# Tile transposes as pairs of 64-row halves, with a new order of the five engine queues

## The chip, the cores and the metric

The kernel runs on one core of one Trainium2 chip. A core has five engines with a queue of instructions each: TensorE (PE: matmuls, with weight loads listed apart as PEld), VectorE (DVE), ScalarE (ACT), GpSimd (POOL) and SyncE (SP, which here issues the DMAs). The metric is the device time of one execution in microseconds. Before the change the median of 3 runs was 202.53 us (202.29 to 202.89).

## What is computed

A transformer layer on x of 2048 rows (tokens) by 448 columns, in bf16. First linear attention with 16 heads of 28 columns, then a gated MLP of width 1792. Cut to what matters:

```python
h  = x + attention(layernorm(x))
h2 = h + mlp(layernorm(h))

# attention
q, k, v = split(x @ wqkv)                       # 16 heads of 28
pq, pk  = q @ w_phi, k @ w_phi                  # per head
phi_q   = concat(softmax(pq), softmax(-pq))     # 56 features; phi_k likewise
kv, z   = phi_k^T @ v, sum over rows of phi_k   # over all 2048 rows
o       = (phi_q @ kv) / (phi_q @ z + 1e-6)
return o @ wo

# mlp
return (sigmoid(x @ w_gate) * (x @ w_up)) @ w_down
```

## The kernel before

**Tiles.** The rows are 16 tiles of 128 (t = 0 to 15), in four chunks of 512 (c = 0 to 3). The 448 columns are the contraction of most products. They are laid out in four blocks of 128 partitions, some of which hold 64 rows that another block repeats, and nearly all products are made as two matmuls of 64 rows that run beside each other in the upper and lower half of TensorE's array (functions `both` and `pair`, lines 304 to 323). A product of two outputs comes as an op "a" (output 1 from the lower 64 rows, output 2 from the upper) and an op "b" (the halves exchanged). The code lets b start only when a's matmuls have ended, since the two write each other's bank from the other half (`crosses`, line 74, and `needs_wait`, line 86); what stands between a and b in the queue fills that time.

**The first half.** For each tile: the layernorm's statistics (`bst`, `agg` on DVE), the reciprocal root (`pow1` on POOL), the normalized tile (`xn`, on DVE or POOL, lines 564 to 584), its transpose (`xT`), the products with the folded k weight and v weight (`ppa/ppb`, `vva/vvb` for tiles 0 to 3, `pva/pvb` from tile 4), two exponentials on ACT (`ek`, lines 669 to 673), the softmax's sum, reciprocal and product (`ss`, `rs` on DVE, `phi` on DVE or POOL, lines 674 to 689), the copy of v out of PSUM (`v1`), and the sum over tiles of phi^T v (`kva`, `kvb`, lines 691 to 703), which stays in PSUM banks 6 and 7 until tile 15 is in. The folded weights of q are made by `w2m1_0` to `w2m1_3` with 128 rows and copied by `w2e1`. The q products of a chunk are `pqa/pqb`, with exponentials `eq` on ACT (lines 711 to 723).

**The second half.** `kvz` copies the finished kv out of PSUM. For each tile `num` (line 774) makes the numerators and denominators, DVE makes from them `rsm`, `qq`, `b`, `c` and `rden` (lines 798 to 806), `o` is the quotient (DVE or POOL, lines 808 to 813), `oT` its transpose. `woa/wob` multiply by wo; for tiles 0 and 1 the residual x is added on TensorE. Then the second layernorm (`h`, `bs2`, `sq`, `ve`, `pow2`, `nm`, `hn`), its transpose `hT`, the gate and up products (`ga`, `gb`), the sigmoid as a tanh on ACT (`sig`), the product on DVE (`hh`), the down products (`dn`, `dp`, `dm`, `dl`) and the last sum (`fin`, `out`).

**Transposes.** Tiles from 4 on (xT) and from 2 on (oT, hT) are transposed by DMA, issued from SP's queue. The first ones are transposed on TensorE by `pe_transpose` (lines 533 to 541): four transposes of 128 by 128 into one PSUM bank, and one copy from there into SBUF by ACT or DVE. These are xT0 to xT3, oT0, oT1, hT0 and hT1, each an op of its own with its copy `xT0e` and so on.

**What sets the order.** The program is a graph of named ops (class `Graph`, line 19). Each op names what it reads and writes, and from that come the semaphores between engines. The order of each engine's queue is written out by hand in `ORDER` (lines 223 to 288), a list of names for each engine; some ops can stand on either of two engines, and the list that names them decides. An engine never passes an op that waits. Two ops, `wwo` and `wgu` (line 896), emit no instruction and only hold the waits for the wo and for the gate and up weights. `PACE` (line 289) adds one more wait: the load `ld_wg1` on SP waits for `kva14`, and as SP's queue is in order, so do the loads behind it.

Of the kernel before, what the change touches and what calls it, by code (L numbers as in the profile page):

```python
# [18 lines left out]
class Graph:  # L19
# [90 lines left out]
    def emit(self, nc):  # L110
# [85 lines left out]
P = 128  # L196
# [83 lines left out]
    ),  # L280
    "pool": (
# [753 lines left out]
```

## Time and profile before

| | |
|---|---|
| runs before | 202.29, 202.53, 202.89 us |
| the profiled execution | 202.7 us, of which 200.8 us from its first to its last instruction (the span) |
| granted TensorE clock | 1.000 over the span |
| instructions | 5854 |
| DMA | 16.26 MB in 32490 packets |
| DMA transposes, issue to landing (median) | xnT<-xn_pad 2.6 us, oT<-o_pad 2.5 us, xnT<-hn_pad 2.5 us |

The times in the profile count from the first instruction. A row of a timeline gives the start, the duration, the engine, the line of the code, the operation, and output<-inputs by the program's names with their shapes; rows of the same kind that follow each other are merged with their count. In square brackets stands how long the engine had been idle and what ended it. A row of the chain gives start, length and what ran: the chain is followed back from the last instruction to whatever released each step. Matmuls are pipelined: one of 512 columns lasts some 0.35 us from its start to its end, but the next starts much sooner, so that the distance from start to start tells what a group costs. The line of nearly all matmuls is 309, that of the helper `both`, so the names of the tiles tell them apart; line 538 is `pe_transpose`, line 531 the copy out of PSUM.

### The profile page before, as it was taken

What the parts mean: (1) busy time and instruction counts of PE and PEld (TensorE: products, weight loads), DVE (VectorE), ACT (ScalarE), POOL (GpSimd) and SP (SyncE); (2) the same over time, 40 slices, a digit from 0 to 9 for tenths busy, and PEclk for the clock granted to TensorE, in tenths of its full rate; (3) what the DMA queues carried; (4) which work ended last, traced back from release to release, by engine and by line L of the source; (5) the groups of instructions that cost most, each with busy time, mean ns of one, the idle gap of its engine ahead of it and who ended that gap; (6) DMA issues with size and microseconds to landing.
All of it is one profiled execution on the core that took longest, in us unless ns stands there. A gap on an engine that the chain in (4) does not pass through costs nothing.

```text
span 200.8 us, 5854 instructions
## 1 busy us (share of the span) xinstructions
PE 195.5 (97%) x2516; PEld 114.4 (57%) x2516; DVE 132.0 (66%) x308; ACT 89.4 (45%) x174; POOL 56.2 (28%) x95
## 2 busy tenths in 40 slices
PE   7999999999999999999999999999999999999995
PEld 4835556565568778787444444555555555554443
DVE  5999999978888986576569877346332422272224
ACT  2668988898883451434232432324323212222220
POOL 5779948633343207510170110001400000000000
PEclk9999999999999999999999999999999999999999
DMA  6965346749984230360015220020312000004002
GB/s 157 316 140 129 54 83 76 221 144 302 309 206 66 52 57 15 66 82 3 0 29 124 56 42 10 20 58 26 65 38 52 0 3 2 0 3 137 0 3 91
DMA packets 32490, 16.26 MB, mean 81 GB/s; under 512 B 24720, under 2 KB 31568, under 8 KB 32464
## 3 DMA queue, kind: packets, MB, share of 16 engines
q1 hardware_dynamic: 32336, 15.86, 33.7%
q8 instruction: 20, 0.33, 0.7%
q14 instruction: 6, 0.05, 0.1%
q10 hardware_dynamic: 128, 0.03, 0.1%
HBM read 8.34 MB, written 1.84 MB: 51 GB/s over the span
## 4 chain that ended last, share of the span: by engine, by line
PE 92%; ACT 3%; DMA 2%; issue 1%; SPq 1%; DVE 0%
PE psum L309 84%; PE psum L954 5%; DMA wk_sb<-in_A_wqkv_dram 2%; ACT hhT L671 1%; ACT eq L721 1%; ACT hhT L672 1%; PE psum L524 1%; PE psum L538 1%; PE psum L612 1%; SPq L413 1%; PE psum L599 0%; ACT xnT L531 0%; ACT v L531 0%; DVE x_sb L961 0%
## 5 line engine op out<-in xcount | busy, mean ns | idle before, releaser
L309 PE MATMUL psum<-xnT,wu_sb 64*128 64x512 bf16 (+1 forms) x490 | 93.6, 333 | 0.0
L309 PE MATMUL psum<-xnT,wg_sb 64*128 64x512 bf16 (+1 forms) x490 | 93.5, 333 | 0.1
L925 ACT ACTIVATE sg_sb<-psum 128x512 bf16<-128x512 f32 x56 | 33.2, 596 | 90.1 <-PE psum L309 89.5
L926 DVE SCALAR_TENSOR_TENSOR hhT<-sg_sb,psum 128x512 bf16<-128x512 bf16 x56 | 37.7, 684 | 52.1 <-ACT sg_sb L925 51.7
L309 PEld LDWEIGHTS psum<-xnT,wg_sb 64*128 64x128 bf16 x490 | 44.6, 94 | 20.9 <-DVE hhT L926 2.5
L309 PEld LDWEIGHTS psum<-xnT,wu_sb 64*128 64x128 bf16 x490 | 44.7, 94 | 13.9
L309 PE MATMUL psum<-wd_sb,hhT 64*128 64x448 bf16 x336 | 37.3, 349 | 0.0
L309 PEld LDWEIGHTS psum<-wd_sb,hhT 64*128 64x128 bf16 x336 | 17.8, 94 | 14.2 <-DVE x_sb L836 0.5
L309 PE MATMUL psum<-Wk,xnT 64*128 64x448 bf16 x112 | 22.2, 350 | 0.5 <-ACT hhT L672 0.2
L309 PE MATMUL psum<-wv_sb,xnT 64*128 64x448 bf16 x112 | 22.3, 351 | 0.1
L810 POOL TENSOR_TENSOR o_pad<-c_sb,rden 128x448 bf16<-128x448 bf16 x11 | 10.2, 935 | 28.5 <-DVE rden L806 28.4
L675 DVE TENSOR_REDUCE ss<-hhT 128x32 f32<-128x896 bf16 x16 | 16.8, 1060 | 0.2 <-ACT hhT L672 0.2
L721 ACT ACTIVATE eq<-psum 120x1024 bf16<-120x1024 f32 x16 | 15.6, 1030 | 0.6 <-PE psum L309 0.4
L685 POOL TENSOR_TENSOR phi<-hhT,rs 128x896 bf16<-128x896 bf16 x8 | 13.6, 1710 | 5.6 <-DVE rs L681 3.4
L309 PE MATMUL psum<-xnT,Wq 64*120 64x512 bf16 x112 | 14.8, 383 | 0.3 <-ACT eq L721 0.2
L845 POOL TENSOR_SCALAR ve<-ssq 128x1 f32<-128x1 f32 x11 | 2.2, 201 | 41.8 <-ACT junk L842 41.5
L309 PE MATMUL psum<-wo_o,oT 64*128 64x448 bf16 x56 | 13.2, 350 | 0.0
L309 PE MATMUL psum<-wo_e,oT 64*128 64x448 bf16 x56 | 13.2, 349 | 0.0
L961 DVE SCALAR_TENSOR_TENSOR x_sb<-psum,x_sb 128x448 bf16<-128x448 f32 (+2 forms) x17 | 9.4, 592 | 2.9 <-PE psum L954 1.6
L954 PE MATMUL psum<-wd_sb,hhT 128*128 128x448 bf16 (+2 forms) x70 | 11.2, 316 | 0.0
L309 PEld LDWEIGHTS psum<-Wk,xnT 64*128 64x128 bf16 x112 | 7.8, 94 | 5.8 <-PE psum L309 1.0
L671 ACT ACTIVATE hhT<-psum 128x448 bf16<-128x448 f32 x16 | 8.8, 553 | 4.4 <-PE psum L309 4.2
(105 smaller groups left out, 234.4 us busy)
## 6 DMA issues: line engine op xcount, KB each, us to landing
out_dram<-x_sb SPq DMA_DIRECT2D x15, 112.0 KB, 1.8
x_sb<-in_A_x_dram SPq DMA_DIRECT2D x7, 224.0 KB, 4.2
wd_sb<-in_B_w_down_dram SPq DMA_DIRECT2D x7, 224.0 KB, 5.1
wg_sb<-in_B_w_gate_dram SPq DMA_DIRECT2D x3, 448.0 KB, 5.8
wu_sb<-in_B_w_up_dram SPq DMA_DIRECT2D x3, 448.0 KB, 5.7
wv_sb<-in_A_wqkv_dram SPq DMA_DIRECT2D x2, 224.0 KB, 4.7
wk_sb<-in_A_wqkv_dram SPq DMA_DIRECT2D x2, 196.0 KB, 4.1
wo_e<-in_A_wo_dram SPq DMA_DIRECT2D x1, 336.0 KB, 3.3
```

Source lines behind the costliest of these rows:

```text
L309: p = e.matmul(o, lhsT=w, rhs=r, start=st, stop=sp, tile_position=(row, 0))
L413: return op(eng, name, lambda e: e.dma_start(dst, src), r=r, w=w, dma="in" if eng == "sp" else "ain", nring=48 if eng == "sp" else 8, kb=kb)
L671: e.activation(ek[:, s, :, 0, :], src, ACT.Exp)
L675: op("dve", "ss%d" % t, lambda e: e.tensor_reduce(ss[:, s, :].rearrange("p (b h) -> p b h", h=2), eks.rearrange("p b (d h) -> p b h d", h= ...
L685: return e.tensor_tensor(phi[:, sp, :, :, :].rearrange("p b a n -> p (b a) n")[:, :, 0:56].rearrange("p b (d h) -> p b d h", h=2), eks.rea ...
L721: op("act", "eq%d_%d%s" % (c, i, "pm"[sg]), lambda e, sg=sg: e.activation(eq[c][:, sg, 2 * i:2 * i + 2, :].rearrange("p g n -> p (g n)"), ...
L810: return e.tensor_tensor(o_pad[:, t % NO, off:off + D].rearrange("p (h d) -> p h d", h=H), c_sb[:, t % NS, :, 0:DH], rden[:, t % NS, :][:, ...
L845: op(("pool", "dve"), "ve%d" % t, lambda e: e.tensor_scalar(ve2[:, t:t + 1], ssq2[:, t:t + 1], 1.0 / D ** 3, EPS, op0=ALU.mult, op1=ALU.ad ...
L925: op("act", "sig" + nm, lambda e: e.activation(sg_sb[:, k, 0:W], bk(bg)[:, 0:W], ACT.Tanh, scale=0.5), r=[B(bg)], w=[("sg", k)])
L926: op("dve", "hh" + nm, lambda e: e.scalar_tensor_tensor(out=dst, in0=sg_sb[:, k, 0:W].rearrange("p (f n) -> p f n", n=N), scalar=1.0, in1= ...
L954: p = e.matmul(bk(b)[:, lo:hi], lhsT=hb[:, ff, TS(t)], rhs=wd_sb[:, ff, lo:hi], start=ff == 0, stop=ff == FT - 1)
L961: op("dve", "fin%d%s" % (t, nm), lambda e: e.scalar_tensor_tensor(out=h_sb[:, t, lo:hi], in0=bk(b)[:, lo:hi], scalar=0.5, in1=h_sb[:, t, l ...
```

## The change

Four things are changed.

1. The transposes of tiles 2 and 3 (xT2, xT3), of o tiles 0 and 1, and of hn tiles 0 and 1 are made by a new function `pair_transpose`. One op for both tiles makes 16 transposes of 64 rows by 128 columns instead of 8 of 128 by 128: the 64 lower rows of every block go to one bank, the 64 upper rows to the next, in two halves of the array. Two copies follow, one for the lower rows of both tiles, one for the upper rows. Whoever reads one of these tiles now waits for both copies. xT0 and xT1 stay as they were.
2. `ld_wg1` waits for `kva12` instead of `kva14`.
3. In SP's queue `ld_wd2` moves behind the DMA transposes oT2 and oT3, so that five down loads stand behind those and not four.
4. The queues of ACT, PE, DVE and POOL are put in another order up to about the products of tiles 4 to 7; the rest is as before. Some ops change their engine.

The functions (the keys of a tile's transposes become two, `XT(t)` and `OT(t)`, at every reader; these lines are left out):

```diff
+        def pair_transpose(names, srcs, banks, dst, rkeys, wkeys):
+            ps = [bk16(b)[:, 0:512] for b in banks]
+
+            def f(e):
+                for i, tile in enumerate(srcs):
+                    for kt, src in enumerate(tile):
+                        o = slice((i * KT + kt) * 64, (i * KT + kt + 1) * 64)
+                        for h, rows in enumerate((LO, HI)):
+                            p = e.transpose(ps[h][:, o], src[rows], ident[rows, rows], tile_position=(64 * h, 0))
+                return p
+            op("pe", names[0], f, r=["ident"] + rkeys, w=[B(b) for b in banks], rows=64, half={b: h for h, b in enumerate(banks)})
+            for h in range(2):
+                evac(names[h] + "e", dst[h], ps[h].rearrange("p (t k s) -> p t k s", t=2, k=KT), B(banks[h]), [k[h] for k in wkeys])
...
-            if t < 4:
+            if t in (2, 3):
+                if t == 3:
+                    v = xnT[0][:, :, 2 * P:4 * P].rearrange("p k (t h s) -> p h t k s", t=2, h=2)
+                    pair_transpose(("xT2", "xT3"), [[xn_pad[:, u % NX, kt * P:(kt + 1) * P] for kt in range(KT)] for u in (2, 3)], (6, 7),
+                                   [v[:, 0], v[:, 1]], [("xn", 2 % NX), ("xn", 3 % NX)], [XT(2), XT(3)])
+            elif t < 2:
...
+                if t == 1:
+                    v = oT[:, 0:2, :, :].rearrange("p t k (h s) -> p h t k s", h=2)
+                    pair_transpose(("oT0", "oT1"), [[o_pad[:, u, kt * P:(kt + 1) * P] for kt in range(KT)] for u in (0, 1)], (2, 3),
+                                   [v[:, 0], v[:, 1]], [("opad", 0), ("opad", 1)], [OT(0), OT(1)])
...
+            if t == 1:
+                v = hnT[0][:, :, 0:2 * P].rearrange("p k (t h s) -> p h t k s", t=2, h=2)
+                pair_transpose(("hT0", "hT1"), [[hn_pad[:, u, kt * P:(kt + 1) * P] for kt in range(KT)] for u in (0, 1)], (0, 1),
+                               [v[:, 0], v[:, 1]], [("hn", 0), ("hn", 1)], [XT(0), XT(1)])
...
-PACE = {"ld_wg1": "kva14"}
+PACE = {"ld_wg1": "kva12"}
```

The queues, cut to the stretches that the prediction speaks of (SP; ACT up to the exponentials of chunk 3; PE up to tile 0's gate products; the parts of DVE and POOL):

```diff
 sp:
-ld_wu3 ld_wd0 ld_wd1 ld_wd2 oT2 oT3 ld_wd3 ld_wd4 ld_wd5 ld_wd6 oT4
+ld_wu3 ld_wd0 ld_wd1 oT2 oT3 ld_wd2 ld_wd3 ld_wd4 ld_wd5 ld_wd6 oT4
 act:
-ek0 xT3e ek1 v1_0 v1_1 nm1_6 ek2 ek3 v1_2 w2e1_1 v1_3 nm1_8 w2e1_0 v1_4 ek4 w2e1_2 ek5 v1_5 w2e1_3 v1_6 ek6
+ek0 ek1 v1_1 v1_0 ek2 w2e1_1 v1_2 ek3 v1_3 w2e1_0 v1_4 ek4 ek5 v1_5 w2e1_2 w2e1_3 v1_6 ek6
...
-ek14 ek15 v1_14 v1_15 eq0_1m eq0_1p eq1_0p kvzA kvzB eq1_0m eq1_1p eq1_1m eq2_0m oT0e eq2_0p eq2_1m eq2_1p h1 h0
+ek14 ek15 v1_14 v1_15 eq0_1p eq0_1m eq1_0m kvzB kvzA eq1_0p eq1_1m eq1_1p eq2_0p oT0e oT1e eq2_0m eq2_1m eq2_1p h1 h0
 pe:
-ppa0 ppb0 warm9 xT2 xT3 vva0 vvb0 ppa2 ppb2 vva2 seed vvb2 w2m1_0 w2m1_1 kva0 pva4 kvb0 pvb4 pva5 w2m1_2 w2m1_3 pvb5
+ppa0 ppb0 warm9 xT2 vva0 vvb0 ppa2 w2m1_1 ppb2 vva2 vvb2 seed w2m1_0 w2m1_3 pva4 kva0 pvb4 pva5 kvb0 kva1 pvb5 w2m1_2
...
-pva15 kvb9 kva10 pvb15 pqa0_1 kvb10 kva11 pqb0_1 kvb11 kva12 pqa1_0 kvb12 kva13 pqb1_0 kvb13 kva14 wwo kvb14 kva15 kvb15
-qs pqa1_1 num0 num1 pqb1_1 pqa2_0 num2 pqb2_0 pqa2_1 oT0 oT1 num3 pqb2_1 woa0 wob0
-pqa3_0 num4 pqb3_0 pqa3_1 pqb3_1 num5 hT1 hT0 woa2 ga0_2 ga0_0 ga0_1 num6
+pva15 kvb9 kva10 pvb15 kvb10 kva11 pqa0_1 kvb11 kva12 pqb0_1 pqa1_0 kvb12 kva13 pqb1_0 kvb13 kva14 kvb14 kva15 kvb15
+qs pqa1_1 num0 pqb1_1 num1 pqa2_0 num2 pqb2_0 pqa2_1 oT0 pqb2_1 num3 woa0 wob0
+pqa3_0 num4 pqb3_0 pqa3_1 pqb3_1 num5 hT0 woa2 ga0_2 ga0_0 ga0_1 num6
 dve:
-bst4 xn2 agg5 agg4 agg7 bst6 xT2e agg6 ss0 bst8 rs0
+bst4 xn2 agg4 agg5 bst6 bst11 xT3e xT2e agg6 agg7 ss0 bst10 rs0
...
-rs5 xn11 ss6 xn12 rs6 ss7 phi5 phi6 xn14 rs7 ss8 ss9 rs8 ss10 rs9 ss11 rs10 ss12 v1_13 rs11 ss13 rs12 phi11 rs13 phi12
+xn11 agg15 phi3 rs5 ss7 ss6 xn12 ss8 rs6 xn14 rs7 phi6 ss9 ss10 rs8 rs9 phi8 rs10 ss11 rs11 ss12 ss13 phi11 rs12 rs13 phi12
...
-qq2 b2 c2 oT1e rsm3 rden2
+qq2 o1 b2 c2 rsm3 rden2
...
-b4 hn1 c4 hn0 rden4 rsm5 hT1e qq5 hT0e b5 c5 rsm6 rden5 qq6 b6 c6 hh0_0
+b4 c4 hn1 hn0 rsm5 qq5 hT0e hT1e rden4 b5 c5 rsm6 qq6 b6 rden5 c6 hh0_0
 pool:
-pow1_6 xn5 xn6 phi0 xn7 pow1_8 xn8 phi2 xn10 xn9 phi4 pow1_12 xn13 phi7 xn15 phi8 phi9 phi10 phi13 o0 o1 o2 o3
+pow1_6 nm1_6 xn6 xn5 phi0 xn7 nm1_8 pow1_8 phi2 xn8 xn9 xn10 phi4 pow1_12 phi5 xn13 phi7 xn15 phi9 phi10 phi13 o0 o2 o3
...
-pow2_6 pow2_5 nm5 hn5 o9 hn6 ve7 pow2_4 hn4 pow2_7 hn7
+ve6 pow2_5 pow2_4 nm5 hn4 hn5 pow2_6 o8 o9 hn6 pow2_7 hn7
```

More of the change, by code (lines that the diff above doesn't have):

```diff
@@ L531, in evac, with XT, OT @@
             op(("act", "dve"), name, (lambda e: e.copy(dst, src), lambda e: e.tensor_copy(dst, src)), r=[rkey], w=[wkey])
+        def XT(t):
+            return [("xnT", t, 0), ("xnT", t, 1)]
+        def OT(t):
+            return [("oT", t, 0), ("oT", t, 1)]
+        def pair_transpose(names, srcs, banks, dst, rkeys, wkeys):
[10 more added lines that the diff above has]
+                evac(names[h] + "e", dst[h], ps[h].rearrange("p (t k s) -> p t k s", t=2, k=KT), B(banks[h]), [k[h] for k in wkeys])
         def pe_transpose(name, srcs, bank, dst, rkey, wkey):
@@ L578, in xnorm @@
             op(("act", "dve", "pool"), "xn%d" % t, (fa, fd, fp), r=[("x", t), ("rst1", a), need], w=[("xn", s)])
-            if t < 4:
+            if t in (2, 3):
[4 more added lines that the diff above has]
+            elif t < 2:
                 pe_transpose("xT%d" % t, [xn_pad[:, s, kt * P:(kt + 1) * P] for kt in range(KT)], 6 + t % 2,
-                             xnT[0][:, :, TS(t)], ("xn", s), ("xnT", t))
+                             xnT[0][:, :, TS(t)], ("xn", s), XT(t))
             else:
                 op("sp", "xT%d" % t, lambda e: e.dma_start_transpose(out=xnT[t // 4][:, :, TS(t)], in_=xn_pad[:, s, :]),
-                   r=[("xn", s)], w=[("xnT", t)], dma="tr", nring=64)
+                   r=[("xn", s)], w=[XT(t)], dma="tr", nring=64)
         for ts in ([0], [1], [2], [3], [4, 5], [6, 7], [8, 9, 10, 11], [12, 13, 14, 15]):
@@ L654, in proj @@
             pairop("pva%d" % t, "pvb%d" % t, pair(bk(bp)[:, 0:D], bk(bv)[:, 0:D], x(t), x(t), wk2, wv),
-                   [("xnT", t)] + W2k + wv_keys, bp, bv)
+                   [XT(t)] + W2k + wv_keys, bp, bv)
         def proj2(nm, t, b, w, r):
             pairop("%sa%d" % (nm, t), "%sb%d" % (nm, t), pair(bk(b)[:, 0:D], bk(b + 1)[:, 0:D], x(t), x(t + 1), w, w),
-                   [("xnT", t), ("xnT", t + 1)] + r, b, b + 1)
+                   [XT(t), XT(t + 1)] + r, b, b + 1)
         def vcopy(t):
@@ L714, in pq @@
                           lambda h, k: xnT[c][h, k, :], lambda h, k: xnT[c][h, k, :])
-            r = W2q + [("xnT", 4 * c + j) for j in range(4)]
+            r = W2q + [XT(4 * c + j) for j in range(4)]
             op("pe", "pqa%d_%d" % (c, i), f1, r=r, w=[B(b), B(b + 1)], rows=64, half={b: 0, b + 1: 1})
@@ L819, in otrans @@
             if t < 2:
-                pe_transpose("oT%d" % t, [o_pad[:, so, kt * P:(kt + 1) * P] for kt in range(KT)], 2 + t % 2, oT[:, so, :, :],
-                             ("opad", so), ("oT", so))
+                if t == 1:
+                    v = oT[:, 0:2, :, :].rearrange("p t k (h s) -> p h t k s", h=2)
+                    pair_transpose(("oT0", "oT1"), [[o_pad[:, u, kt * P:(kt + 1) * P] for kt in range(KT)] for u in (0, 1)], (2, 3),
+                                   [v[:, 0], v[:, 1]], [("opad", 0), ("opad", 1)], [OT(0), OT(1)])
             else:
                 op("sp", "oT%d" % t, lambda e: e.dma_start_transpose(out=oT[:, so, :, :], in_=o_pad[:, so, :]),
-                   r=[("opad", so)], w=[("oT", so)], dma="tr", nring=64)
+                   r=[("opad", so)], w=[OT(so)], dma="tr", nring=64)
         def resid(t, b, ha=False):
@@ L856, in resid @@
                 op("sp", "hT%d" % t, lambda e: e.dma_start_transpose(out=hnT[c][:, :, TS(t)], in_=hn_pad[:, s, :]),
-                   r=[("hn", s)], w=[("xnT", t)], dma="tr", nring=64)
+                   r=[("hn", s)], w=[XT(t)], dma="tr", nring=64)
         def htrans(t):
-            s = t % NH
-            pe_transpose("hT%d" % t, [hn_pad[:, s, kt * P:(kt + 1) * P] for kt in range(KT)], t, hnT[0][:, :, TS(t)], ("hn", s), ("xnT", t))
+            if t == 1:
+                v = hnT[0][:, :, 0:2 * P].rearrange("p k (t h s) -> p h t k s", t=2, h=2)
+                pair_transpose(("hT0", "hT1"), [[hn_pad[:, u, kt * P:(kt + 1) * P] for kt in range(KT)] for u in (0, 1)], (0, 1),
+                               [v[:, 0], v[:, 1]], [("hn", 0), ("hn", 1)], [XT(0), XT(1)])
         def wout(t):
@@ L877, in fb @@
                             xp(t, 2, HI, False) + [(bk(2)[:, 0:D], ot(t)(HI, k), wo_e[HI, k, :], False, k == 2) for k in (0, 1, 2)])
-            r = [("oT", t % NO), ("oT", (t + 1) % NO)] + wo_keys + ([("x", t), ("x", t + 1), "ident"] if ha else [])
+            r = [OT(t % NO), OT((t + 1) % NO)] + wo_keys + ([("x", t), ("x", t + 1), "ident"] if ha else [])
             op("pe", "woa%d" % t, fa, r=r, w=[B(2), B(3)], rows=64, half={2: 0, 3: 1})
@@ L889, in part @@
                 return [(bk(b)[:, 0:D], oT[h, so, k, :], w[h, k, :], first and k == ks[0], not first and k == ks[-1]) for k in ks]
-            r = [("oT", so)] + wo_keys
+            r = [OT(so)] + wo_keys
             op("pe", "woa%d" % t, lambda e: both(e, part(LO, lo, True), []), r=r, w=[B(b)], rows=64, half={b: 0})
@@ L904, in gate_up @@
             ns = slice((t0 % 4) * P, (t0 % 4) * P + N)
-            hk = [("xnT", t) for t in range(t0, t0 + n)]
+            hk = [XT(t) for t in range(t0, t0 + n)]
             two = n == 2
```

94 rows, old and new, of the table ORDER are left out of this document.

## The prediction

> **What bounds the kernel now.** I read the page's engine rows and its chain first, then the busy time by stretch, the chain in order of time, and the timelines of TensorE, VectorE and GpSimd wherever the diff moves something. All durations are of the one profiled execution.
>
> ```profile
> PE 195.5 (97%) x2516; PEld 114.4 (57%) x2516; DVE 132.0 (66%) x308; ACT 89.4 (45%) x174; POOL 56.2 (28%) x95
> ```
> ```profile
> PE 92%; ACT 3%; DMA 2%; issue 1%; SPq 1%; DVE 0%
> ```
>
> TensorE is full and ends last, so at first sight only fewer TensorE cycles count. The stretches correct that:
>
> ```profile
> 9.00:43.40 34.40, 33.84 (x537) 19.29 (x534) 33.94 (x72) 28.82 (x66) 25.41 (x25) 1.00 0.59 131
> 43.40:58.20 14.80, 14.08 (x268) 8.49 (x262) 11.85 (x34) 13.07 (x18) 5.53 (x7) 1.00 0.93 245
> ```
>
> The columns are length, then busy time of PE, PEld, DVE, ACT and POOL. Up to 43.4 us DVE is as full as PE (33.94 of 34.40 us, 0.46 us idle). In the second stretch it is ACT (13.07 of 14.80). Two engines are close behind PE there.
>
> ```profile
> 12.32 0.48 ACT xnT L531
> ```
> ```profile
> 16.58 0.44 ACT hhT L671
> 17.02 0.44 ACT hhT L672
> 17.45 0.43 ACT v L531
> ```
> ```profile
> 47.20 1.95 ACT eq L721 x2
> ```
> ```profile
> 58.21 65.46 PE psum L309 x960
> ```
>
> The chain leaves PE for the copy of xT3, for ek3 and the copy v1_2 behind it, and for the two exponentials of pq1_1; from 58.21 us it is matmuls for 65 us without a break. What is gained before 58 us reaches the end one to one, and so does any new wait after it.
>
> **The transposes, on PE.**
>
> ```profile
> 50.20 0.62 PE L538 MATMUL psum<-ident,o_pad 128*128 128x128 bf16 x8
> 50.75 0.40 PE L309 MATMUL psum<-kvz,eq 56*128 56x60 bf16 x16
> 50.99 0.84 PE L309 MATMUL psum<-xnT,Wq 64*120 64x512 bf16 x6
> ```
> ```profile
> 57.18 0.39 PE L309 MATMUL psum<-kvz,eq 56*128 56x60 bf16 x16
> 57.59 0.62 PE L538 MATMUL psum<-ident,hn_pad 128*128 128x128 bf16 x8
> ```
>
> Starts tell PE's cost better than durations, since matmuls overlap. Eight full transposes take 50.75 - 50.20 = 0.55 us. The new pair is 16 matmuls of 64 rows and 64 columns, two row halves side by side. The trace has none of these; the nearest row is the quotient's product, 16 of 56 rows and 60 columns, 50.99 - 50.75 = 0.24 us. Before the transposes the same 16 take 57.59 - 57.18 = 0.41 us: 0.17 us is PE running empty before it goes from 64 rows to 128. So a pair saves 0.31 us, and 0.17 more where both neighbours have 64 rows: 0.48 for oT and hT, and 0.31 for xT, which still follows a 128-row warm-up. That is 1.3 us of PE; bounds are zero gain (halves one after the other) and this. How much of it ends last is settled by stage.
>
> [...]
>
> **Stage A, to the last kv product (44.4 us).**
>
> ```profile
> 17.72 0.66 ACT L629 CAST Wq<-psum 128x224 bf16<-128x224 f32 x2
> ```
>
> ACT loses the 0.48 us copy of xT3 above, and pva4 waits for v1_2 behind such a weight copy (w2e1_1, 0.66 us) where ek3 was (0.88 in the chain): 0.7 us earlier in all. PE also puts a second filler between the a and b halves of several pairs, where it waited some 0.1 us, and loses the empty wait op wwo: 0.3. PE alone could come about 1.0 us earlier. DVE can't:
>
> ```profile
> 10.63 0.40 DVE L573 TENSOR_SCALAR xn_pad<-x_sb,mv,rst 128x512 bf16<-128x512 bf16 x1
> ```
> ```profile
> 11.78 0.42 DVE L531 COPY xnT<-psum 128x512 bf16<-128x512 bf16 x1
> ```
> ```profile
> 36.53 0.62 DVE L531 CAST v<-psum 128x448 bf16<-128x448 f32 x1
> ```
> ```profile
> 42.22 1.14 DVE L685 TENSOR_TENSOR phi<-hhT,rs 128x896 bf16<-128x896 bf16 x2
> ```
> ```profile
> 43.69 0.76 PE L309 MATMUL psum<-v,phi 64*128 64x58 bf16 x24 [0.15 <-PE psum L309]
> ```
>
> DVE gains the second xT copy (0.42), gives v1_13 to ACT (0.62), and swaps phi5 for phi8 (nothing): 0.2 us less. phi15 ended at 42.22 + 1.14 = 43.36. It ends at 43.16 with the old idle time, at 42.70 with none; I take the middle, 42.95. kvb14, kva15 and kvb15 (the 24 matmuls, to 44.45) need phi14 and phi15. After phi15 at 42.95, kva15 comes at 43.2 and kvb15 ends about 43.85. **Stage A: -0.6 us**, bounds -0.1 (DVE idles 0.3 more than before) and -1.0 (PE's own).
>
> **Stage B, to the output projection woa0.**
>
> ```profile
> 49.19 1.07 PE L309 MATMUL psum<-xnT,Wq 64*120 64x512 bf16 x8 [0.25 <-ACT eq L721]
> ```
> ```profile
> 51.66 0.35 PE L309 MATMUL psum<-x_sb,ident 64*128 64x448 bf16 x2
> ```
>
> num1 moves behind pqb1_1, so the exponentials that pqa2_1 waits for start 0.24 us earlier, and the pair takes 0.48 less of PE. Against that, o1 now stands on DVE ahead of b2 and c2, whose end num3 awaits, and both oT copies stand on ACT one behind the other, 0.48 us apart as in the chain above. I work out woa0 at 51.52 where it was 51.66: **-0.14 us**, bounds 0 (ACT later by one copy) and -0.7 (all of PE's).
>
> **Stage C, to num6.**
>
> ```profile
> 57.61 0.26 DVE L798 RECIPROCAL rsm<-psum 128x16 f32<-128x16 f32 x1 [0.21 <-PE psum L309]
> 58.03 0.43 DVE L531 COPY xnT<-psum 128x512 bf16<-128x512 bf16 x1 [0.15 <-PE psum L538]
> 58.37 0.16 DVE L799 TENSOR_TENSOR qq<-rsm,psum 128x16 f32<-128x16 f32 x1
> 58.44 0.42 DVE L531 COPY xnT<-psum 128x512 bf16<-128x512 bf16 x1
> 58.78 0.63 DVE L801 TENSOR_TENSOR b_sb<-psum,qq 128x464 bf16<-128x464 f32 x1
> 59.44 0.64 DVE L804 TENSOR_TENSOR c_sb<-b_sb,psum 128x464 bf16<-128x464 bf16 x1
> ```
> ```profile
> 60.31 0.41 PE L309 MATMUL psum<-kvz,eq 56*128 56x60 bf16 x16
> ```
>
> PE would be 0.48 us early, but the copies aren't: DVE does rsm5 and qq5 (behind num5), then hT0e, hT1e, rden4, b5, c5. From num5's start, the copies end after 1.56 us (before 58.86 - 57.18 = 1.68), c5 after 2.95 (before 2.90), and num6, which needs c5's banks, comes after 3.01 instead of 60.31 - 57.18 = 3.13. **-0.12 us**, bounds +0.1 and -0.48. From num6 to the first h product DVE's row of work is the same length, since the moved rden5 fits where c6 waits for b6.
>
> **Costed at nothing.** The weight loads:
>
> ```profile
> 43.57 0.47 SPq L413 DMA_DIRECT2D wg_sb<-in_B_w_gate_dram  x1
> ```
> ```profile
> DMA to landing us min/median/max: 2.9/5.8/8.3
> ```
>
> With kva12 moved forward too, ld_wg1 and all that SP holds behind it start some 3 us earlier. The six gate and up loads of that row are issued by 46.8 and land at most 8.3 us later, 55.1; the first gate product runs at 59.01 (the row below), so nothing on PE waits for them before or after.
>
> ```profile
> 59.01 0.27 PE L309 MATMUL psum<-xnT,wg_sb 64*128 64x256 bf16 x1
> ```
>
> oT2 and oT3 go ahead of wd2 and land earlier; wd2 isn't needed before the first down products. If that cover went, woa2 would wait for oT3, and it has 0.5 us to spare, as ga0_2 behind it waits for the copies. The wgu marker moves behind products that wait for the same loads. After 58 us only order changes; PE's sum there is the same.
>
> The sum is -0.6 - 0.14 - 0.12 = -0.86 us. The profiled execution took 202.7 us (span 200.8), so 201.84 for one like it; the median of the runs, 202.53, is 0.17 lower: **201.7 us**.
>
> **Rivals.**
>
> *DVE holds stage A.* Its idle time doesn't shrink, as ss7, ss12 and ss13 now stand before older work and wait for ACT's exponentials. Then stage A gives 0.1 and the whole 0.36: 202.2. For it: DVE's fill above. Against: before, only 0.46 us of waits arose in 34.
>
> *Late transposes, slower than before.* GpSimd takes over o8 and hn4 comes ahead of o9:
>
> ```profile
> 78.05 1.21 POOL L851 TENSOR_SCALAR hn_pad<-x_sb,nm,rst 128x512 bf16<-128x512 bf16 x1 [0.18 <-POOL nm L840]
> 79.23 0.93 POOL L810 TENSOR_TENSOR o_pad<-c_sb,rden 128x448 bf16<-128x448 bf16 x1
> ```
> ```profile
> DMA to landing us min/median/max: 2.4/2.5/4.4
> ```
> ```profile
> 84.70 0.35 PE L309 MATMUL psum<-wo_e,oT 64*128 64x448 bf16 x1
> ```
>
> o9 (0.93) ends about 1.1 us later, near 81.2; its transpose is issued behind that of o8, near 81.6, and lands at 84.1 with the median of 2.5 us and at 86.0 with the longest. woa8, at 84.70, needs it: up to 1.3 us of wait, straight to the end. That is -0.86 + 1.3 = +0.44: **203.0**. It decides from a landing of 3.1 us; below that it costs nothing. For it: the longest landing and GpSimd's row of work. Against: half land within 2.5 us. The same can happen once more:
>
> ```profile
> 19.23 0.77 POOL L576 TENSOR_SCALAR xn_pad<-x_sb,nm,rst 128x512 bf16<-128x512 bf16 x1 [0.17 <-POOL rst L554]
> 20.08 1.69 POOL L685 TENSOR_TENSOR phi<-hhT,rs 128x896 bf16<-128x896 bf16 x1
> ```
>
> xn8 now stands behind phi2 and ends near 22.0 instead of 20.0; pva8, near 24.9, would wait for xT8 if that took over 2.9 us. With both the time goes past 203.1.
>
> *The halves don't run side by side.* Then 16 matmuls cost up to twice 0.24, about the old 0.55 less a little; the copies hide part: 201.9 to 202.3. Against: two row halves run together all over this trace.
>
> [...]
>
> *PE alone sets stages A to C*: the bounds -1.0 - 0.7 - 0.48 sum to -2.2; taken three quarters, since ACT's exponentials stay in B, -1.6: 200.9. For it: PE is at 97%. Against: DVE's rows.
>
> **Chances.** Forecast (201.1 to 202.2) 0.54; DVE holds A 0.15; late transposes 0.18; no side by side 0.05; PE alone 0.08. A measurement of this kernel can tell about 0.3%, 0.6 us, from no change, so faster means below 201.92: 0.45 of the forecast's 0.54, all of PE alone, a fifth of the halves rival, 0.54. Slower means above 203.14: 0.10, the half of late transposes in which both places wait. The rest is 0.36. Leaving out 0.05 below and these 0.10 above, the range is 200.9 to 203.1.
>
> **What would show it.** The pair's 16 matmuls start to next start in 0.25 us; no empty wait of 0.17 before oT and hT; DVE's last phi ends near 42.95 and num6 starts near 59.45. A DVE phi end above 43.3 refutes stage A; copies that take over 0.5 us on DVE refute stage C; a wait at woa8 for oT shows the slower rival.

## The result, and the profile after

The changed kernel takes **204.02 us** (median of 6 runs, 203.67 to 204.55), the kernel before beside it 202.50 (6 runs, 202.29 to 202.89): a ratio of 1.0074, with a 95% interval of 1.0057 to 1.0090. The change costs 1.5 us; the forecast was a gain of 0.86, and the time lies above the range. The profiled execution took 204.1 us, with a span of 202.1, at full clock. Two executions of the experiments below were in a slower state (208.17 us of a_merge19, 205.89 of a_single) and are left out of the medians and ranges.

The page of after, in the rows that answer to those of before: the engines' busy time, and the chain that ended last by engine.

```profile
PE 195.5 (97%) x2540; PEld 112.2 (56%) x2540; DVE 131.6 (65%) x305; ACT 90.1 (45%) x173; POOL 57.8 (29%) x99
PE 74%; DVE 16%; DMA 4%; ACT 2%; issue 1%; SPq 1%; DVEq 0%
```

PE is busy for the same 195.5 us, so the lost time isn't work of PE. The chain has more of DVE (16% for 0%) and of DMA (4% for 2%). The first three lines of PE's waits, longest first, name it (engine and line, what was waited for, us in total, times, longest):

```profile
PE psum L524 <- DVE zero L417: 1.2, 1, 1.2
PE psum L309 <- DMA xnT<-xn_pad: 0.9, 2, 0.5
PE psum L309 <- issue: 0.7, 1, 0.7
```

The first stands at the start of both kernels. The other two are new: PE waits twice for a DMA transpose of xn, and once for something that the view can't name. PE's timeline at these three places shows which operations they are (start, duration, and in brackets the idle time and its releaser):

```profile
22.93 0.36 PE L309 MATMUL psum<-Wk,xnT 64*128 64x448 bf16 x1 [0.42 <-DMA xnT<-xn_pad]
```
```profile
38.31 0.36 PE L309 MATMUL psum<-Wk,xnT 64*128 64x448 bf16 x1 [0.49 <-DMA xnT<-xn_pad]
```
```profile
72.05 0.35 PE L309 MATMUL psum<-wo_e,oT 64*128 64x448 bf16 x1 [0.67 <-issue]
```

They are pva7, which needs xT7, pva15, which needs xT15, and woa6, which needs oT7. Start to start, beyond the usual step (0.19 us behind such products, 0.11 behind a gate product), PE loses 0.58, 0.65 and 0.83 us there. The third releaser is a DMA too, as the landing of oT7 shows. For each kernel, the DMA view of oT7's flight (queues with packets and MB; then the issues in that stretch with their time from issue to landing), first before, 67.30 to 69.85 us:

```profile
q1 hardware_dynamic: 544, 0.13, 26.0%
issues: line engine op xcount, KB each, median us to landing
oT<-o_pad SPq DMA_TRANSPOSE x1, 2.4
```

and after, 67.8 to 72.0 us:

```profile
q1 hardware_dynamic: 1397, 0.34, 42.7%
q8 instruction: 1, 0.02, 1.4%
issues: line engine op xcount, KB each, median us to landing
oT<-o_pad SPq DMA_TRANSPOSE x1, 4.1
xnT<-hn_pad SPq DMA_TRANSPOSE x1, 2.9
```

(The last line is another transpose, hT2, which was issued behind it.) The same transpose, oT7, lands after 4.1 us where it took 2.4, and one packet of a second queue is in its flight: q8, kind "instruction". After's xT7 and xT15 show the same, 4.6 and 4.3 us for 2.5 before, each with such a packet; here the view of xT7's flight in after:

```profile
q1 hardware_dynamic: 1059, 0.26, 74.5%
q8 instruction: 1, 0.02, 2.8%
q14 instruction: 1, 0.01, 0.7%
issues: line engine op xcount, KB each, median us to landing
xnT<-xn_pad SPq DMA_TRANSPOSE x1, 4.6
```

**Where the time went, by stage.** The table gives the start of an operation's first matmul, in us of the span.

| | ppa0 | pva4 | pva8 | pva15 | kvb15 | woa0 | num6 | woa4 | woa6 | woa8 | dl15_0 |
|---|---|---|---|---|---|---|---|---|---|---|---|
| before | 9.56 | 18.02 | 25.50 | 37.76 | 44.17 | 51.66 | 60.31 | 66.44 | 69.98 | 84.70 | 197.47 |
| after | 9.16 | 17.24 | 25.13 | 38.31 | 44.64 | 52.22 | 60.87 | 66.84 | 72.05 | 86.02 | 198.78 |
| difference | -0.40 | -0.78 | -0.37 | +0.55 | +0.47 | +0.56 | +0.56 | +0.40 | +2.07 | +1.32 | +1.31 |

At ppa0 nothing of the change has run; the 0.40 us is where the second load of Wk happened to land sooner (at 5.57 us for 6.34), so the loss behind it is larger than the last column says. The other profiles below stand 0.1 to 0.5 us ahead of before at ppa0 too, all but a_pace14. (woa6 stands two gate products later in the new order, which is why a part of +2.07 is given back by woa8.) Behind woa8 the two run alike.

### The profile page after: what moved, and what is told of

The parts are those of the page before. It is cut to its first block, busy times and chain, and to the rows that moved or that the text cites. A ratio compares the mean times of both kernels' runs of the same rounds, so it can differ in the third digit from the quotient of the medians.

```text
span 202.1 us, 5905 instructions
## 1 busy us (share of the span) xinstructions
PE 195.5 (97%) x2540; PEld 112.2 (56%) x2540; DVE 131.6 (65%) x305; ACT 90.1 (45%) x173; POOL 57.8 (29%) x99
## 3 DMA queue, kind: packets, MB, share of 16 engines
q1 hardware_dynamic: 32336, 15.86, 33.7%
## 4 chain that ended last, share of the span: by engine, by line
PE 74%; DVE 16%; DMA 4%; ACT 2%; issue 1%; SPq 1%; DVEq 0%
PE psum L309 69%; PE psum L983 5%; DVE ss L700 5%; DVE st L565 4%; DMA x_sb<-in_A_x_dram 2%; DMA xnT<-xn_pad 2%; ACT eq L746 1%; DVE rs L706 1%; DVE phi L710 1%; DVE c_sb L829 1%; DVE b_sb L826 1%; DVE xnT L531 1%; SPq L413 1%; DVE xn_pad L593 1%; ACT kvz L779 1%
## 5 line engine op out<-in xcount | busy, mean ns | idle before, releaser
L309 PE MATMUL psum<-Wk,xnT 64*128 64x448 bf16 x112 | 22.7, 350 | 1.1 <-DMA xnT<-xn_pad 0.9
L309 PE MATMUL psum<-wv_sb,xnT 64*128 64x448 bf16 x112 | 22.8, 351 | 0.1
L835 POOL TENSOR_TENSOR o_pad<-c_sb,rden 128x448 bf16<-128x448 bf16 x10 | 9.6, 960 | 30.5 <-DVE rden L831 30.5
```

Source lines behind the costliest of these rows:

```text
L309: p = e.matmul(o, lhsT=w, rhs=r, start=st, stop=sp, tile_position=(row, 0))
L835: return e.tensor_tensor(o_pad[:, t % NO, off:off + D].rearrange("p (h d) -> p h d", h=H), c_sb[:, t % NS, :, 0:DH], rden[:, t % NS, :][:, ...
```

## What the instruction packets are: two theories

Queue q8 is the same on the pages of before and after:

```profile
q8 instruction: 20, 0.33, 0.7%
```

Twenty packets of 16,384 bytes are 0.33 MB. TensorE runs 2540 matmuls and as many weight loads, 5080 instructions, or 254 for each packet; the next engine, DVE, runs 305. In the same way b_merge19 below, which runs 38 instructions fewer than before (4994 for 5032), has one packet fewer:

```profile
q8 instruction: 19, 0.31, 0.6%
```

So I take q8 to be TensorE's program being fetched, a packet about every 127 matmuls (2540 / 20). The page gives q8 (0.7%) and q1, the queue of the transposes (33.7%), as shares of the same 16 DMA engines. A packet lasts about 1 us (0.93 to 1.75 in after).

**Theory F:** a fetch that falls into the flight of a DMA transpose delays its landing by up to 2 us (xT7 has 4.6 for 2.5); how it would do so no run here shows. Where the fetches fall would be set by TensorE's position in its program. Three pairs add 24 matmuls, and the order moves the transposes: so the change would have moved fetches onto transposes that PE needs at once.

**Rival O:** the new order issues these transposes later relative to their need and loads SP's queue more; long landings are chance, as before had them too (oT4 4.4, oT5 4.2, xT13 3.9 us, none of which cost PE more than 0.15). **Rival P:** the pairs themselves cost time. **Rival L:** the earlier weight loads lengthen the landings.

## The experiments

Each kernel was run beside the kernel before. The ratio is to that, with its 95% interval.

| kernel | median us | runs | ratio |
|---|---|---|---|
| b_split29 | 204.74 | 204.48 to 205.69 | 1.0110 (1.0073 to 1.0148) |
| b_pair | 204.73 | 204.52 to 207.27 | 1.0130 (1.0064 to 1.0195) |
| b_pair_merge19 | 202.40 | 202.08 to 203.34 | 0.9998 (0.9978 to 1.0019) |
| a_merge19 | 204.88 | 203.85 to 205.59 | 1.0103 (1.0052 to 1.0154) |
| a_merge19_pace14 | 202.59 | 201.74 to 203.96 | 1.0017 (0.9994 to 1.0039) |
| a_pace14 | 203.80 | 203.68 to 203.93 | 1.0070 (1.0050 to 1.0090) |
| b_merge19 | 202.73 | 202.31 to 203.56 | 1.0018 (1.0003 to 1.0033) |
| a_fill | 203.95 | 203.35 to 205.11 | 1.0080 (1.0053 to 1.0106) |
| b_split12 | 203.64 | 202.82 to 205.46 | 1.0064 (1.0037 to 1.0092) |
| a_merge14_pace14 | 202.79 | 202.40 to 204.49 | 1.0021 (1.0003 to 1.0040) |
| a_single | 202.84 | 202.46 to 203.73 | 1.0025 (1.0008 to 1.0041) |
| a_later_fold | 202.40 | 202.18 to 202.81 | 0.9990 (0.9979 to 1.0002) |

### b_split29: the kernel before, its stream 29 matmuls longer

```diff
-for i, (n, size) in enumerate(((4, 512), (1, 512), (1, 128), (2, 128), (1, 128), (6, 128), (4, 128), (6, 128), (8, 128), (2, 128))):
+for i, (n, size) in enumerate(((16, 128), (4, 128), (1, 128), (2, 128), (1, 128), (6, 128), (4, 128), (12, 64), (16, 64), (2, 128))):
```

> The kernel before, with its warm-up matmuls cut into more and smaller ones: 29 more matmuls with the same columns in all, so that everything TensorE runs behind them stands 58 instructions later in its stream. Theory F (TensorE's instruction fetches of 16 KB, one for every 256 instructions or so, delay a DMA transpose that is under way by about 1.7 us): the fetches come some 1.5 to 2 us earlier relative to the work, the one that came at 70.9 us now falls into the landing of oT7, and woa6 waits for it: 203.5 to 204.3 us, all of the loss at woa6. Rival O (the new order is what makes the waits: transposes are issued later relative to their need): nothing here changes the order, 202.3 to 202.8 us.

Measured: 204.74 us, 2.2 slower than before, though nothing but idle warm-ups was cut smaller. The chain of b_split29 in order of time, around woa6, and the DMA view of oT7's flight (67.7 to 72.0 us):

```profile
58.62 11.92 PE psum L309 x224
70.53 1.50 issue
72.03 7.97 PE psum L309 x128
```
```profile
q1 hardware_dynamic: 657, 0.16, 18.7%
q8 instruction: 1, 0.02, 1.4%
issues: line engine op xcount, KB each, median us to landing
xnT<-hn_pad SPq DMA_TRANSPOSE x2, 2.5
oT<-o_pad SPq DMA_TRANSPOSE x1, 4.2
```

woa6 waits 1.5 us for oT7, with the fetch in its flight, as F said: before's order, and after's wait. Up to pva12 (32.38 us) b_split29 stands a constant 0.37 us ahead of the profiled before, so the cut warm-ups cost nothing by themselves. Rival O had given 202.3 to 202.8. The time is above F's 203.5 to 204.3, as a second part of the loss was not expected: PE stops for half a microsecond within num0's sixteen matmuls, where no semaphore is waited for.

```profile
45.59 0.38 PE L309 MATMUL psum<-kvz,eq 56*128 56x60 bf16 x14
46.46 0.43 PE L309 MATMUL psum<-kvz,eq 56*128 56x60 bf16 x18 [0.49 <-issue]
```

### b_pair and b_pair_merge19: the pairs alone, in before's order

In b_pair the transposes are as in after, all orders as before:

```diff
-warm9 xT2 xT3 vva0
+warm9 xT2 vva0
...
-pqa2_1 oT0 oT1 num3
+pqa2_1 oT0 num3
...
-num5 hT1 hT0 woa2
+num5 hT0 woa2
```

> The kernel before with the three pair transposes alone; order, pace and queues as before. The stream of TensorE has 8 matmuls more behind xT2, 16 behind oT0, 24 behind hT0. Theory F: the pairs save 0.3 to 0.5 us, but by the 24 added matmuls the fetch near 70.9 us falls into the landing of oT7, which costs about 1.6: 203.4 to 204.0 us, and the wait stands at woa6. Rival O (the order made the change slower): 201.9 to 202.4 us, no wait at woa6. Rival P (pairs themselves cost time): slower, but with the time lost at the pairs or their copies.

b_pair_merge19 also joins the warm-ups, 19 matmuls fewer:

```diff
-((4, 512), (1, 512), (1, 128), (2, 128), (1, 128), (6, 128), (4, 128), (6, 128), (8, 128), (2, 128))
+((4, 512), (1, 512), (1, 128), (1, 256), (1, 128), (2, 384), (1, 512), (2, 384), (2, 512), (1, 256))
```

> The same as b_pair (before's order, three pair transposes), with the warm-up matmuls joined into fewer and longer ones: 19 fewer with the same columns, so that the stream at the output projection is only 5 matmuls longer than before's. Theory F: no fetch falls on a transpose that TensorE waits for: 201.9 to 202.3 us, faster than both, no wait at woa6. Rival O: the same as b_pair within 0.2 us. Rival P: as b_pair, slower than before.

Measured: 204.73 and 202.40 us. The same order and the same pairs differ by 2.3 us through 19 warm-up matmuls that do no work. PE's waits, first of b_pair, then of b_pair_merge19:

```profile
PE psum L309 <- issue: 1.4, 1, 1.4
PE psum L309 <- DMA oT<-o_pad: 1.1, 1, 1.1
```
```profile
PE psum L309 <- DMA oT<-o_pad: 0.4, 1, 0.4
```

In b_pair the 1.4 us is at woa6 (oT7 landed after 4.05 us), and the 1.1 us at woa2: oT3 took 4.66, behind oT2 with a fetch in its flight. (oT2 landed 2.0 us behind the weight load ahead of it, where before and b_pair_merge19 have 0.6.) For this second wait b_pair is above F's 203.4 to 204.0. b_pair_merge19 has no wait at woa6. F holds, and O, which had both alike near 202, falls as the cause here; so does P, as the time isn't lost at the pairs. But b_pair_merge19, a little above F's 201.9 to 202.3, isn't faster than before either, where 0.2 to 0.5 us was expected: without a wait at woa6 the pairs are worth about nothing.

### a_merge19, a_merge19_pace14, a_pace14: after, with the fetches moved

a_merge19 is after with the joined warm-ups above; a_pace14 is after with the pause of the loads as before; a_merge19_pace14 has both.

```diff
-PACE = {"ld_wg1": "kva12"}
+PACE = {"ld_wg1": "kva14"}
```

> The kernel after, with 19 fewer warm-up matmuls of the same columns in all. Theory F: the fetches come some 1.2 us later relative to the work; the long landings of xT7, xT15 and oT7 move to other transposes (by a rough shift of the fetch times to xT12, xT13 and oT5, which have more room): the waits of 0.6 us at pva7, pva15 and woa6 go, smaller ones may come at pva12 and woa4, 202.6 to 203.6 us. Rival O: 203.7 to 204.4 us with the three waits in their places.

> The kernel after with 19 fewer warm-up matmuls of the same columns, as in a_merge19, and the pause of the weight loads back at tile 14's kv product, as before. In a_merge19 TensorE stood still for 3.9 us in the middle of num2 while the fetch of its instructions came at 48.75 us behind the weight loads that fill the DMA engines from 42 to 53 us. Theory F (the fetch, here stuck behind loads): with the loads some 1.5 to 2 us later the fetch that TensorE needs at 47.5 us goes ahead of them, no stop in num2, and none of the three waits of after: 201.6 to 202.4 us. Rival: the merged warm-ups themselves cost time (the clock, or work that comes too early): again above 203.5 us.

> The kernel after with nothing changed but the pause of the weight loads, back at tile 14's kv product. The stream of TensorE is the same instruction for instruction. Theory F: the fetches near 19.7, 36 and 70 us stand where they stood, and so do the waits for xT7, xT15 and oT7: 203.4 to 204.2 us. Rival L (the earlier weight loads are what lengthens the landings): the waits go or shrink, 202.0 to 202.8 us.

a_merge19 took 204.88 us, outside what F gave; the three waits were gone (kvb15 at 43.45 us, 0.7 ahead of before), but PE stopped in the middle of num2. The busy time by stretch (length; then PE, PEld, DVE, ACT, POOL, the granted clock, the DMA engines' share, GB/s):

```profile
46.00:47.50 1.50, 1.50 (x36) 0.99 (x31) 1.47 (x4) 1.19 (x2) 0.00 (x0) 1.00 1.05 256
47.50:51.40 3.90, 0.01 (x1) 0.00 (x0) 0.74 (x3) 0.75 (x1) 0.94 (x1) 0.87 1.02 293
51.40:58.00 6.60, 6.60 (x70) 3.93 (x69) 3.17 (x10) 3.74 (x5) 0.53 (x1) 0.56 0.14 47
```
```profile
51.40 0.38 PE L309 MATMUL psum<-kvz,eq 56*128 56x60 bf16 x8 [3.89 <-issue]
```

For 3.9 us PE does nothing with half of a product still to run, while the DMA engines are full (1.02) with weight loads; the fetch that follows the one at 39.7 us appears at 48.75. The granted clock falls to a half (0.50 from 52 to 56 us) only 3 us into the stop, at 50.35 us, and is full again at 57.2, so it can't have caused the stop. This profiled execution took 208.17 us, with a granted clock of 0.56 from 51.40 to 58.00; the other three took 203.85 to 205.59 and have no profile.

The place of such stops settles what they are. Besides b_split29 and a_merge19, a_single below has one. PE stops in three different products (num0, num2, pqa2_0), but each time after exactly 1473 instructions of PE's queue in the trace (matmuls, weight loads and their semaphore waits). And it goes on 1.4 us behind the end of the same packet of q8, the fifth in the span: the packet's end and the next matmul are at 45.06 and 46.46 us in b_split29, 50.06 and 51.40 in a_merge19, 47.25 and 48.63 in a_single. In the other eleven profiles the 1474th instruction starts 1.47 to 3.3 us behind that packet, and none stops there. So PE waited for its program.

With the loads' pause back at tile 14 there is no such stop, and a_merge19_pace14 takes 202.59 us, 1.4 less than after with the same columns of work; a little above the 202.4 that F allowed. (It waits 0.9 us for the last transposed load of Wq.) a_pace14, whose stream is after's, stays at 203.80, as F had said: the pause alone is worth next to nothing, and L falls. In its profile xT7 (4.8 us) and oT7 (4.0) were late as in after; xT15 was not, its fetch coming 0.2 us before the landing.

### b_merge19: the control

> The kernel before with 19 fewer warm-up matmuls of the same columns: the control for b_pair_merge19, which has the pair transposes besides. Theory F: the fetches come later relative to the work, the one at 64.4 us may pass oT5's landing, nothing new is hit before woa8: 202.1 to 202.6 us. The difference to b_pair_merge19 is then what the pairs alone are worth: by the forecast 0.2 to 0.5 us, by the stages of b_pair_merge19 near nothing.

202.73 us, a little above what F gave. In its profile woa2 waits 0.5 us for oT3, as the weight loads ahead of it landed 0.9 us later than in before. Against b_pair_merge19 (202.40) the pairs may be worth 0.3 us, but the intervals of the two ratios overlap.

### a_fill: work put into the waits

```diff
-pvb6 pva7 pqa0_0 pvb7 pva8 kvb2 pvb8
+pvb6 kvb2 pva7 pqa0_0 pvb7 pva8 pvb8
...
-pvb14 pva15 kvb9 kva10 pvb15
+pvb14 kvb9 kva10 pva15 pvb15
...
-gb0_10 woa6 num9 wob6 ga0_12 ga0_13 gb0_11 gb0_12
+gb0_10 gb0_11 num9 woa6 wob6 ga0_12 ga0_13 gb0_12
```

> The kernel after with three waits given work that is ready, in TensorE's order alone: kvb2 ahead of pva7, kvb9 and kva10 ahead of pva15, gb0_11 and num9 ahead of woa6; as many instructions as after. Theory F (the late landings of xT7, xT15 and oT7 are the whole loss): the landings stay as late, but 0.2 + 0.45 + 0.5 us of the waits are filled: 202.7 to 203.2 us. Rival O (what PE does first sets the rest through other engines): 203.6 to 204.3 us.

203.95 us in the median, 203.35 in the profiled execution: 0.1 or 0.75 below after. The median lies in rival O's range (203.6 to 204.3) and not in F's. The landings stay late (4.2, 4.1 and 4.0 us), and PE's view of waits lists no DMA any more. But the moves cost time of their own: from each start to the next, gb0_11, woa6 and ga0_13 take 0.61, 0.99 and 0.67 us, where they take 0.33, 0.75 and 0.44 in after, as num9 doesn't follow at once behind gb0_11, and nothing stands between woa6 and wob6, or ga0_13 and gb0_12, any more. That is 0.75 us in all. The runs spread over 1.8 us, so this kernel is inconclusive on the size.

### b_split12: half a shift

```diff
-((4, 512), (1, 512), (1, 128), (2, 128), (1, 128), (6, 128), (4, 128), (6, 128), (8, 128), (2, 128))
+((16, 128), (1, 512), (1, 128), (2, 128), (1, 128), (6, 128), (4, 128), (6, 128), (8, 128), (2, 128))
```

> The kernel before with only its first warm-up cut from 4 matmuls into 16 of the same columns: 12 matmuls more, where b_split29 had 29. Theory F (a fetch of TensorE's instructions delays the transpose under way): 12 matmuls shift the fetch near 70.9 us by some 0.7 us, which leaves it behind oT7's landing at 69.8: no wait at woa6, 202.2 to 202.9 us. Rival W (cut warm-ups cost time by themselves, by the clock or by their number): about 12/29 of the loss of 2.2 us, 203.2 to 203.6 us.

203.64 us: F's number was wrong, and the median falls on that of rival W. The places don't: up to pva8 the kernel stands a constant 0.42 us ahead of before, then PE waits at pva11, at kva8 (for a phi of GpSimd) and at woa2, nowhere near the warm-ups.

```profile
PE psum L309 <- DMA oT<-o_pad: 1.3, 1, 1.3
PE psum L309 <- DMA xnT<-xn_pad: 1.1, 1, 1.1
PE psum L309 <- POOL phi L685: 0.6, 1, 0.6
```

xT11 took 5.2 us with two fetches in its flight (q8 and the 8 KB one of q14), oT3 5.0 us with one. woa6 is free, as F had said of it. That profiled execution was the slowest of ten (205.46, the fastest 202.82). So F fits the places in this one execution, but my shifted fetch times don't forecast which transpose is hit to better than half a microsecond.

### a_single: after without the pairs

after's orders, queues and pause, with the six full transposes of before.

```diff
-warm9 xT2 vva0
+warm9 xT2 xT3 vva0
...
-pqa2_1 oT0 pqb2_1
+pqa2_1 oT0 oT1 pqb2_1
...
-num5 hT0 woa2
+num5 hT0 hT1 woa2
```

> The kernel after with its order, queues and pause, but with the six full transposes instead of the three pairs: 8 matmuls fewer behind xT2, 16 behind oT0, 24 behind hT0. Theory F: the fetch near 70 us comes 1.5 us later relative to the work and misses oT7, so the 0.7 us at woa6 goes, against 0.2 to 0.4 us that the pairs save; the early fetches move by 0.5 us alone and can still hit xT7: 203.0 to 204.0 us. By the prediction's working, in which pairs only save: 204.4 to 205.0 us.

202.84 us, a little below F's 203.0 to 204.0: taking the pairs, which PE runs in half the time, out of after makes it about 1 us *faster*. The DMA view of 67 to 72 us has no instruction packet:

```profile
q1 hardware_dynamic: 1632, 0.39, 39.2%
issues: line engine op xcount, KB each, median us to landing
oT<-o_pad SPq DMA_TRANSPOSE x2, 2.4
xnT<-hn_pad SPq DMA_TRANSPOSE x1, 2.4
```

Its profiled execution (203.73, the slowest of the nine) has the third of the stops told of under a_merge19:

```profile
48.63 0.43 PE L309 MATMUL psum<-xnT,Wq 64*120 64x512 bf16 x2 [0.53 <-issue]
```

### a_merge14_pace14 and a_later_fold: looking for the order's own worth

a_merge14_pace14 leaves the short warm-ups alone (14 fewer matmuls):

```diff
-((4, 512), (1, 512), (1, 128), (2, 128), (1, 128), (6, 128), (4, 128), (6, 128), (8, 128), (2, 128))
+((4, 512), (1, 512), (1, 128), (2, 128), (1, 128), (2, 384), (4, 128), (2, 384), (2, 512), (2, 128))
```

> The kernel after with 14 fewer warm-up matmuls and the loads' pause as before: like a_merge19_pace14, whose fetch at 22.4 us still fell on xT8, with that fetch some 0.3 us earlier, between the landing of xT7 (near 20.9) and the issue of xT8 (near 21.8). Theory F: pva8 waits no longer, and the order's own gain up to the last kv product, 0.5 us in a_merge19, stands: 201.7 to 202.4 us. Rival: as a_merge19_pace14, 202.3 to 202.9 us, or new waits on oT2 and oT3, above 203 us.

a_later_fold is a_merge19_pace14 with one move:

```diff
-ppa2 w2m1_1 ppb2 vva2 vvb2 seed w2m1_0
+ppa2 ppb2 vva2 w2m1_1 vvb2 seed w2m1_0
```

> a_merge19_pace14 (after's order, 19 fewer warm-up matmuls, pause of the loads as before) with one product of the folded weights, w2m1_1, three products later, behind vva2. In after's order it stands at 13.9 us and needs the last transposed load of Wq, which landed at 13.0 us in after, but at 14.5 and 15.1 us where a fetch of TensorE's instructions at 12.5 or 13.0 us fell on it, and TensorE waited up to 1.2 us there. Theory F: this wait goes, pva4 stands near 17.4 us in every execution, the fetch near 21.6 us passes between xT7 and xT8 as in a_merge19, and the order's own 0.5 us up to the last kv product stays: 201.6 to 202.3 us, below both kernels. Rival O (the order is no faster by itself): 202.4 to 202.9 us like a_merge19_pace14.

202.79 and 202.40 us, both outside what F gave and inside what the rivals gave, by which the order is no faster by itself. In a_merge14_pace14 the fetch at 13.05 us held the last transposed load of Wq, which the new order needs early, and one at 57.2 us held oT2 and oT3:

```profile
PE psum L309 <- DMA oT<-o_pad: 1.3, 1, 1.3
PE psum L637 <- DMA WqT<-in_A_wqkv_dram: 1.2, 1, 1.2
```

In a_later_fold that wait is gone, pva4 stands at 17.04 us and pva8 at 24.46, 0.5 us better than its start explains; but xT12 is hit (3.7 us), pva12 waits, and at kvb15 (43.69) it has only the 0.5 us by which it started ahead. No version was found that beats before by more than the measurement tells.

## Why the prediction was wrong, point by point

The step that failed is one that the sum doesn't have: the landings of the DMA transposes. The working left them as they were and gave the 24 added matmuls no cost beyond PE's own time. The runs showed three landings of 4.1 to 4.6 us instead of 2.5, each with a fetch of TensorE's program in its flight, and they cost PE 0.58, 0.65 and 0.83 us. By the prediction's own steps:

- **The pairs on PE: half right.** Three rows of after, each 16 matmuls, with the start of what follows: 0.23, 0.22 and 0.25 us, as the forecast 0.24.

```profile
11.19 0.41 PE L547 MATMUL psum<-ident,xn_pad 64*128 64x64 bf16 x16
11.42 0.37 PE L309 MATMUL psum<-wv_sb,xnT 64*128 64x448 bf16 x2
```
```profile
50.56 0.41 PE L547 MATMUL psum<-ident,o_pad 64*128 64x64 bf16 x16
50.78 0.64 PE L309 MATMUL psum<-xnT,Wq 64*120 64x512 bf16 x4
```
```profile
58.15 0.41 PE L547 MATMUL psum<-ident,hn_pad 64*128 64x64 bf16 x16
58.40 0.35 PE L309 MATMUL psum<-wo_e,oT 64*128 64x448 bf16 x1
```

  That is 14 to 16 ns a matmul, and not the up to twice 0.24 us of halves that run one after the other. What failed was what a pair is worth: the copies, oT3's landing and ACT end last there, and b_pair_merge19 is not faster than before. The empty 0.17 us ahead of hT, which the working put to the change from 64 rows to 128 and counted as saved, was misread. From num5's start to hT's it is 0.41 us in before, after and b_pair_merge19 alike, and what releases hT is ACT's second exponential of pq3_0, whose banks the transposes write: it ends at 57.53, 58.10 and 57.04 us, and hT starts 0.06, 0.05 and 0.06 later. So a pair is worth 0.31 us of PE at most, and no run here shows what a change of rows costs.
- **Stage A, "-0.6 us": the step that failed first.** DVE's phi15 ended at 43.74, beyond the 43.3 that was to refute it; kvb15 came at +0.47 instead of -0.6.

```profile
42.58 1.16 DVE L710 TENSOR_TENSOR phi<-hhT,rs 128x896 bf16<-128x896 bf16 x2
```

  The working took the landings of the xn transposes as they were. Two were late by about 2 us (0.58 and 0.65 us of PE). Here the new order has a part in the loss, as rival O has it: from the issue to the moment that PE is ready, xT7 has 4.1 us in after and 5.2 in before, xT15 3.7 and 4.3, so before's order would have covered landings of 4.6 and 4.3 us, or nearly. (For oT7 the room grew, from 2.6 to 3.4.) Up to pva4 the order gained 0.4 us behind ppa0, where 0.7 was reckoned. Without these hits the order is faster in parts: a_merge19 reached kvb15 0.7 us ahead of before, 0.15 of it by its start. In a_later_fold, where xT12 was hit, nothing was left.
- **Stage B, "-0.14", and C, "-0.12":** +0.09 and 0.00 (woa0 and num6 in the table). DVE's two copies took 0.38 us each, under the 0.5 that was to refute stage C; their end still set the first gate product.

```profile
58.60 0.76 DVE L531 COPY xnT<-psum 128x512 bf16<-128x512 bf16 x2
59.51 0.27 PE L309 MATMUL psum<-xnT,wg_sb 64*128 64x256 bf16 x1 [0.18 <-DVE xnT L531]
```

- **"After 58 us only order changes; PE's sum there is the same": failed.** The sum is the same, but from num6 to the end 0.75 us was lost: woa6's wait for oT7, 0.83 in itself. This, stage A (1.07 us off), B (0.23) and C (0.12) make up the 2.17 us between the forecast -0.86 and the +1.31 of the table.
- **The weight loads at nothing:** right for the change as it stood (a_pace14 203.80), but only by the place of one fetch: with 19 warm-ups fewer the early pause goes with 2.3 us (a_merge19 against a_merge19_pace14).
- **The rival "late transposes"** had the right kind of event, and the wrong cause and places. It treated 4.4 us as the rare end of a spread ("half land within 2.5 us") and put it at oT9 and xT8, which landed in 2.4 us in after. Here the three long landings had a fetch in their flight, and the place of the fetch moved with the program: with 29 matmuls more one was in the flight of oT7 (b_split29, 4.2 us). The term that the sum lacked is the length of TensorE's instruction stream.

What stays open: what the new order would be worth with no hit at all (a_merge19 and a_later_fold bound stage A between -0.6 and 0), and a rule that tells beforehand which transpose a given stream hits. F is shown by the places of the waits; its times were inside the range that was given in one kernel of the twelve (a_pace14).

## What to carry to other kernels

An instruction that costs nothing on its engine still has a place in the program, and in this kernel the program's fetches delayed the data's transfers: adding 24 matmuls, or 29 that do no work, moved it by 2 us (b_pair 204.73, b_split29 204.74, before 202.5). Before a gain or loss of 1% is put down to an edit, run the edit again with the stream shifted by a dozen idle instructions. Look at the packets of kind "instruction" in the flight of every transfer that is needed at once, and give a transpose like these 4.5 us, not its median of 2.5, or work that can go ahead of it.

## What the runs showed of the hardware

- Over the 14 profiles, 117 DMA transposes had a TensorE fetch begin within 2.45 us of their issue: median landing 3.45 us, longest 4.8. Of 415 others the median is 2.48 (oT2 and oT3, which queue behind weight loads, are left out). Neither side is clean: 20 of the 117 landed within 2.6 us, and 41 of the others took over 3 us. Of these, ten are oT4 (up to 6.0 us), 17 had an 8 KB packet of the other instruction queue, q14, begin in that time, and 9 were issued while a fetch of q8 ran.
- A fetch can itself be late: TensorE stood still for 0.49 us (b_split29), 0.53 us (a_single) and 3.89 us (a_merge19; the DMA engines' share was 1.02 then, of weight loads) in the middle of an operation, with no semaphore to wait for, each time after the same 1473 instructions, and went on 1.4 us behind the end of the packet. In the view of waits such a stop reads "issue".
